# Attention and two MoE stages on one core: the last chunk's down product by seven block products

## The chip, the cores and the metric

One core of a Trainium2 chip runs the whole program. The metric is the device time of an execution in microseconds; the time before is the median of three runs.

## The reference

Clustered attention feeds a gated MoE, and that feeds a second MoE, the stage at hand. It has 1536 tokens of width 512 and four experts with 1024 hidden units:

```python
p = domain_probs / (domain_probs.sum(-1, keepdims=True) + 1e-09)
out = np.zeros((N, D), dtype=np.float32)
for e in range(E):
    h = np.maximum(x @ w1[e], 0.0)
    out += p[:, e:e + 1] * (h @ w2[e])
```

## The kernel before, in words

**Numbers in two parts.** Every float32 operand of a matmul is kept as a high and a low part (names that end in h and l: `hh`, `hl`, `wdh`, `wdl`), and every product is three matmuls: high by high, high by low, low by high. ScalarE writes a high part by a cast (`hi`, L1117), VectorE the low part by a subtraction (`lo`, L1120).

**Chunks.** The second MoE runs over 16 chunks, (2, 0) to (2, 15): four experts with four pieces of 256 hidden units each. A chunk has an *up* product, which makes the 256 hidden rows for all tokens, and a *down* product, which multiplies them by w2 and adds the result to `acc`, the sum of the whole output in SBUF. Tokens stand in three blocks of 512: blocks 0 and 1 (`tb`) hold the output transposed, with four tiles of 128x512 each; the third block holds it by rows, as four *row blocks* of 128 tokens.

**Seven products.** A 2 by 2 product of blocks is made from seven block products in place of eight, with sums of weight blocks (`ws`, made by `block_sums`, L189) and sums of hidden blocks (`ts`, made in `up_seven`, L1142). Up products of (2, 1) to (2, 15) go this way. Down products of (2, 1) to (2, 14) do so in `down_seven` (L1229): each of the seven `product` calls has 2 x 3 matmuls, and between them stand the four `last_block` calls (L1263), one for each row block, with 6 matmuls each. The last chunk, (2, 15), uses `up_seven` without the hidden sums (`blocks` is false) and then the plain `down` (L1395): row blocks first, then the four tiles of block 1, then those of block 0, the last tile in two halves.

**How results reach `acc`.** In `down_seven` a result is taken out of PSUM by VectorE, which adds it to `acc` (`by_v`, L1250), or by ScalarE, which copies it to a tile `ev`, from which a transfer issued by GpSimd adds it to `acc` in memory (`by_a`, L1256; an *accumulating transfer*). The four row blocks go by ScalarE with the token's share as scale, and an accumulating transfer. `ev` tiles come in turn from a pool with two buffers and one with three. In the plain `down` VectorE adds everything, and SP issues a store of each finished tile to `out` (L1428).

**Order.** The schedule is written by hand: each engine runs its instructions in the order in which the code issues them, and each DMA queue belongs to an engine (SP for loads and stores, GpSimd for accumulating transfers). An instruction that waits keeps those behind it on its engine waiting. `step()` calls put side work, the next weights' casts above all, between the products.

Of the kernel before, what the change touches and what calls it, by code (L numbers as in the profile page):

```python
# [39 lines left out]
def tile_cluster_attention_moe(ctx, tc, qk, vt, cent, consts, wm1, wm2, probs, probs_t, out):  # L40
# [12 lines left out]
    wtie = const.tile([128, NCL], BF16, name="wtie")  # L53
    zero1 = const.tile([128, 1], F32, name="zero1")
    cT = const.tile([128, H, 2, NCL], F32R, name="cT")
    identb = const.tile([128, 128], BF16, name="identb")
# [166 lines left out]
    def w_steps(todo):  # L223

        prev = None
        for k, part, o, _ in todo:
# [5 lines left out]
            blocks = k[1] not in (0, E2 * NC2 - 1) if part == "d" else k[1] > 0  # L232
# [53 lines left out]
    def attention():  # L286
        with ExitStack() as ax:
            qkp = ax.enter_context(tc.tile_pool(name="qkp", bufs=2))
            stg = ax.enter_context(tc.tile_pool(name="stg", bufs=1))
            clp = ax.enter_context(tc.tile_pool(name="clp", bufs=1))  # L290
            sm = ax.enter_context(tc.tile_pool(name="sm", bufs=2))
# [537 lines left out]
    def moe():  # L829
# [9 lines left out]
        prs = ap_.tile([128, 128], F32, name="prs")  # L839
# [4 lines left out]
        late = []  # L844
        x3_t = [hp1.tile([128, 2, 768], F32R, name="xt" + x) for x in "hl"]
# [112 lines left out]
        def third_seven(key):  # L958
# [4 lines left out]
            x = tp.tile([128, 512], F32, tag="sg", name="sx", bufs=3)  # L963
            y = ev_.tile([128, 512], F32, tag="ev", name="sy")
# [13 lines left out]
            A.copy(out=y[:, 256:512], in_=gc)  # L978
# [8 lines left out]
            add(y[:, 256:512], ga)  # L987
# [154 lines left out]
        def up_seven(key):  # L1142


            blocks = key[1] < E2 * NC2 - 1
# [18 lines left out]
            parts = [([t[:, i * 256:i * 256 + 256] for t in f1], g) for i, g in ((0, ga), (1, y[:, 256:512]))]  # L1164
# [10 lines left out]
            if not blocks:  # L1175
                hi(h12, u2)
            next(t3)
            if blocks:
                ts[1] = [wp.tile([128, 512], F32R, tag="wb", name="th", bufs=2) for _ in range(2)]
                minus(m1, u2, m1)  # L1180
                hi(ts[1], m1)
# [9 lines left out]
            if blocks:  # L1191
                lo(ts[1], m1)
                minus(u2, m5, u2)
            relu_lo(key, 0, x)
            if blocks:
                minus(x, m5, m1)
            relu_part(*parts[1])
            if blocks:
                hi(ts[3], u2)
                hi(ts[2], x)  # L1200
                lo(ts[2], x)
                lo(h22, m5)
            else:
                lo(h12, u2)
                lo(h22, m5)
# [323 lines left out]
```

## Time and profile before

| | |
|---|---|
| median of three runs | 1027.23 us (1026.77 to 1029.91) |
| the profiled execution | 1029.32 us, span 1027.5 us |
| PE | busy 1015.4 us, 99% of the span |
| VectorE (DVE), ScalarE (ACT), GpSimd (POOL) | 82%, 62%, 34% |
| chain that ended last | PE 77%, DVE 5%, POOL 5%, DMA 4%, ACT 3% |
| granted TensorE clock | 0.998 of full speed over the span |
| stores to `out` by SP | 11 of 256 KB and 2 of 128 KB |
| accumulating transfers of 256 KB by GpSimd | 164, median 4.7 us to landing |

PE's busy share is that of pipelined matmuls: a matmul of 512 columns has a duration of 0.39 us, while the next one starts 0.23 us after it. Times of rows are counted from the span's start. A store or transfer lands when its completion is signalled.

### The profile page before, as it was taken

What the parts mean: (1) busy time and instruction counts of PE and PEld (TensorE: products, weight loads), DVE (VectorE), ACT (ScalarE), POOL (GpSimd) and SP (SyncE); (2) the same over time, 40 slices, a digit from 0 to 9 for tenths busy, and PEclk for the clock granted to TensorE, in tenths of its full rate; (3) what the DMA queues carried; (4) which work ended last, traced back from release to release, by engine and by line L of the source; (5) the groups of instructions that cost most, each with busy time, mean ns of one, the idle gap of its engine ahead of it and who ended that gap; (6) DMA issues with size and microseconds to landing.
All of it is one profiled execution on the core that took longest, in us unless ns stands there. A gap on an engine that the chain in (4) does not pass through costs nothing.

```text
span 1027.5 us, 15450 instructions
## 1 busy us (share of the span) xinstructions
PE 1015.4 (99%) x5273; PEld 832.2 (81%) x5273; DVE 842.5 (82%) x1583; ACT 637.4 (62%) x1273; POOL 350.6 (34%) x404
## 2 busy tenths in 40 slices
PE   8999999999999999999999999999999999999998
PEld 5787777787888888788888888888888888888886
DVE  7888888898588887878787888898888889888876
ACT  6788778887566555645544656565565656556561
POOL 2856786652200102010100144433344443334430
PEclk9999999999999999999999999999999999999999
DMA  8677968831713525253410176655667665665753
GB/s 209 173 168 154 192 155 186 196 86 51 201 57 99 126 82 107 85 136 86 101 42 21 41 144 123 144 105 115 125 139 154 131 124 105 130 126 124 144 103 122
DMA packets 62101, 126.27 MB, mean 123 GB/s; under 512 B 16064, under 2 KB 21504, under 8 KB 62024
## 3 DMA queue, kind: packets, MB, share of 16 engines
q0 software_dynamic: 35632, 62.93, 33.6%
q1 hardware_dynamic: 26104, 62.30, 20.5%
q8 instruction: 41, 0.67, 0.3%
q14 instruction: 36, 0.29, 0.1%
q10 hardware_dynamic: 288, 0.07, 0.0%
HBM read 69.47 MB, written 3.21 MB: 71 GB/s over the span
## 4 chain that ended last, share of the span: by engine, by line
PE 77%; DVE 5%; issue 5%; POOL 5%; DMA 4%; ACT 3%; SPq 0%; POOLq 0%; ACTq 0%; DVEq 0%
PE pa L1005 17%; PE pd L1377 9%; PE pd L1242 9%; PE pb L275 6%; PE pb L1297 5%; PE pt L1005 5%; PE ps L495 4%; PE pb L1005 4%; PE pa L275 3%; PE ps L472 2%; PE ps L473 2%; PE pd L1421 2%; DMA raw<-in_qk 2%; PE pv L525 2%; PE pv L530 2%
## 5 line engine op out<-in xcount | busy, mean ns | idle before, releaser
L1260 POOL DMA_DIRECT2D acc<-ev x84 | 73.8, 1026 | 188.0 <-ACT ev L1259 186.5
L478 DVE CUSTOM_DVE_ANT_0 junk<-ps,zero 128x768 bf16<-128x768 f32 x96 | 91.0, 948 | 14.4 <-PE ps L473 13.8
L489 ACT ACTIVATE P<-ps,nm 128x768 f32<-128x768 f32 x96 | 87.4, 910 | 12.7 <-DVE nm L478 12.5
L1383 POOL DMA_DIRECT2D acc<-ev x24 | 20.8, 867 | 202.3 <-ACT ev L1382 202.0
L495 PE MATMUL ps<-ident,P 128*128 128x128 f32 x576 | 84.5, 274 | 0.9 <-ACT sc L443 0.9
L514 DVE TENSOR_TENSOR lo<-ps,hi 128x384 fp32r<-128x384 f32 x128 | 68.8, 554 | 10.5 <-ACT hi L500 8.2
L495 PEld LDWEIGHTS ps<-ident,P 128*128 128x128 f32 x576 | 66.0, 141 | 10.2 <-ACT hi L500 2.5
L1253 DVE TENSOR_TENSOR acc<-pd,acc 128x512 f32<-128x512 f32 x112 | 71.7, 682 | 0.0
L472 PE MATMUL ps<-t 80*128 80x512 f32 x192 | 70.5, 367 | 1.2 <-ACT P L489 0.4
L500 ACT CAST hi<-ps 128x384 fp32r<-128x384 f32 x128 | 58.0, 482 | 18.8 <-PE ps L495 18.5
L1268 POOL DMA_DIRECT2D acc<-ev x56 | 48.3, 886 | 61.6 <-ACT ev L1267 58.1
L473 PE MATMUL ps<-t 128*128 128x512 f32 x192 | 62.3, 345 | 0.0
L1005 PE MATMUL pa<-xsh,wuh 128*128 128x512 f32 x150 | 60.5, 404 | 0.1
L337 POOL TENSOR_TENSOR t<-raw,t 64x768 fp32r<-64x768 f32 x26 | 47.4, 1824 | 35.6 <-DVE lo L514 19.2
L1005 PE MATMUL pa<-xsl,wuh 128*128 128x512 f32 x150 | 59.1, 394 | 0.0
L1005 PE MATMUL pa<-xsh,wul 128*128 128x512 f32 x150 | 59.0, 393 | 0.0
L1005 PE MATMUL pa<-xh,wuh 128*128 128x512 f32 x150 | 58.7, 392 | 0.0
L1005 PE MATMUL pa<-xh,wul 128*128 128x512 f32 x150 | 58.6, 390 | 0.0
L1005 PE MATMUL pa<-xl,wuh 128*128 128x512 f32 x150 | 58.3, 389 | 0.0
L1377 PE MATMUL pd<-hl,wdh 128*128 128x512 f32 x144 | 56.2, 390 | 0.2 <-DVE hl L1055 0.2
L1377 PE MATMUL pd<-hh,wdh 128*128 128x512 f32 x144 | 56.1, 390 | 0.0
L1377 PE MATMUL pd<-hh,wdl 128*128 128x512 f32 x144 | 56.1, 389 | 0.0
(318 smaller groups left out, 3287.7 us busy)
## 6 DMA issues: line engine op xcount, KB each, us to landing
acc<-ev POOLq DMA_DIRECT2D x164, 256.0 KB, 4.7
wraw<-in_wm SPq DMA_DIRECT2D x68, 512.0 KB, 3.9
t<-in_qk POOLq DMA_DIRECT2D x13, 768.0 KB, 6.8
t<-in_qk POOLq DMA_DIRECT2D x14, 384.0 KB, 7.9
raw<-in_qk SPq DMA_DIRECT2D x26, 192.0 KB, 6.8
x<-x SPq DMA_DIRECT2D x21, 192.0 KB, 4.9
R<-rd SPq DMA_DIRECT2D x16, 192.0 KB, 5.3
out<-acc SPq DMA_DIRECT2D x11, 256.0 KB, 2.0
```

What stands on the lines that cost most here:

```text
L275: T.matmul(out=ps, lhsT=w[:, o:o + 128], rhs=x, start=(k == 0 and m == 0), stop=(k == 3 and m == 2))
L472: T.matmul(out=ps, lhsT=t2[:, 0, qs], rhs=t2[:, 1, ks], start=True, stop=False)
L473: T.matmul(out=ps, lhsT=t1[:, 0, qs], rhs=t1[:, 1, ks], start=False, stop=True)
L478: V.tensor_tensor_reduce(out=junk, in0=S_t[n], in1=zero1.to_broadcast([128, S]), scale=-0.125, scalar=3.0e38, op0=ALU.add, op1=ALU.min, ac ...
L489: A.activation(out=P_t[n], in_=S_t.pop(n), func=ACTF.Exp, scale=0.125, bias=nm_t.pop(n), accum_out=rs_t[p][:, h, c:c + 1])
L495: T.transpose(ps[:, i * 128:(i + 1) * 128], P_t[3 * u + i][:, j * 128:(j + 1) * 128], ident)
L514: V.tensor_tensor(out=lo, in0=ps, in1=hi.bitcast(F32), op=ALU.subtract)
L1005: T.matmul(out=ps, lhsT=w[:, o:o + 128], rhs=r, start=first and i == 0 and m == 0, stop=i == 1 and m == 2, skip_group_check=not first)
L1242: T.matmul(out=ps[s], lhsT=w[i][:, o + s * 128:o + s * 128 + 128], rhs=x[j], start=first and m == 0, stop=m == 2, skip_group_check=not first)
L1253: V.tensor_tensor(out=y, in0=ps, in1=y, op=ALU.add)
L1260: G.dma_start(out=acc1[:, 2 * half + s, tb * 512:(tb + 1) * 512], in_=ev, accum_op=ALU.add)
L1377: T.matmul(out=ps, lhsT=w[:, o:o + 128], rhs=x[:, f, sl], start=(n == 0), stop=(n == len(terms) - 1))
```

## The change

The last chunk goes by seven in its down product too. Its up product makes the hidden sums, its down weights get their sums (`w_steps`), and `down_seven` has rules for this chunk (`last`): a tile that will not be added to again (`done`) is stored by SP as soon as it is finished; `by_a` tiles that are done are added by GpSimd (an add of 128x512 in SBUF) in place of an accumulating transfer; the first two row blocks still go by ScalarE and an accumulating transfer, with a store behind each; the third and fourth are scaled and added by VectorE, the fourth in two halves. The plain `down` keeps only the form for (2, 0). The third block's two sums (`sx`, `sy`) get tiles of their own in place of buffers of the two `ev` pools. `cT`, `identb` and `wtie` move to a pool that lives only during the attention, and `prs` becomes a part of `sy`.

```diff
@@ w_steps
-            blocks = k[1] not in (0, E2 * NC2 - 1) if part == "d" else k[1] > 0
+            blocks = k[1] > 0
@@ moe, third_seven
+        sums3 = hp1.tile([128, 512], F32, name="sx"), hp1.tile([128, 256], F32, name="sy")
+        prs = sums3[1][:, 0:128]
...
-            x = tp.tile([128, 512], F32, tag="sg", name="sx", bufs=3)
-            y = ev_.tile([128, 512], F32, tag="ev", name="sy")
+            x, y = sums3
@@ up_seven: what stood under "if blocks" stands for every chunk
-            if not blocks:
-                hi(h12, u2)
...
-            if not blocks:
-                c21()
-                lo(h21, t21)
@@ down_seven
+            last = key == chunks[-1]
...
+            def send(half, tb, s, done):
+                if last and done:
+                    SY.dma_start(out=out[4 * tb + 2 * half + s], in_=acc1[:, 2 * half + s, tb * 512:(tb + 1) * 512])
+
-            def by_v(half, tb):
+            def by_v(half, tb, done=False):
                 def finish(ps, s):
                     y = acc1[:, 2 * half + s, tb * 512:(tb + 1) * 512]
                     V.tensor_tensor(out=y, in0=ps, in1=y, op=ALU.add)
+                    send(half, tb, s, done)
                 return finish
 
-            def by_a(half, tb):
+            def by_a(half, tb, done=False):
                 def finish(ps, s):
                     ev = ev_tile()
                     A.copy(out=ev, in_=ps)
-                    G.dma_start(out=acc1[:, 2 * half + s, tb * 512:(tb + 1) * 512], in_=ev, accum_op=ALU.add)
+                    y = acc1[:, 2 * half + s, tb * 512:(tb + 1) * 512]
+                    if last and done:
+                        G.tensor_tensor(out=y, in0=ev, in1=y, op=ALU.add)
+                        send(half, tb, s, done)
+                        return
+                    G.dma_start(out=y, in_=ev, accum_op=ALU.add)
                 return finish
 
             def last_block(t):
                 ps = bank("b")
+                if last and t > 1:
+                    for cs in [slice(0, DM)] if t == 2 else [slice(0, 256), slice(256, DM)]:
+                        y = acc1[:, t, 1024 + cs.start:1024 + cs.stop]
+                        ps = bank("b") if cs.start else ps
+                        rows_(ps[:, cs], h, raw, t, cs)
+                        V.scalar_tensor_tensor(out=y, in0=ps[:, cs], scalar=pn[:, t, e:e + 1], in1=y, op0=ALU.mult, op1=ALU.add)
+                        SY.dma_start(out=out[8 + t, :, cs], in_=y)
+                    return
                 rows_(ps, h, raw, t, slice(0, DM))
                 ev = ev_tile()
                 A.activation(out=ev, in_=ps, func=ACTF.Copy, scale=pn[:, t, e:e + 1])
                 G.dma_start(out=acc1[:, t, 1024:1536], in_=ev, accum_op=ALU.add)
+                if last:
+                    SY.dma_start(out=out[8 + t], in_=acc1[:, t, 1024:1536])
...
             last_block(0)
             product(u, sums, 256, ts[2], False, by_v(0, 1))
...
-            product(q, sums, 768, b22, False, by_a(0, 1))
+            product(q, sums, 768, b22, False, by_a(0, 1, True))
             next(rest)
             last_block(1)
-            product(u, sums, 512, ts[3], False, by_a(1, 1))
+            product(u, sums, 512, ts[3], False, by_a(1, 1, True))
             step()
-            product(q, raw, DM, b21, True, by_v(0, 0))
+            product(q, raw, DM, b21, True, by_v(0, 0, True))
             step()
             last_block(2)
-            product(u, raw, DM + 256, ts[4], False, by_v(1, 0))
+            product(u, raw, DM + 256, ts[4], False, by_v(1, 0, True))
             step()
             last_block(3)
```

Two places of the instruction order follow, with what each instruction waits for in brackets. A name that begins with DMASW is the completion of an accumulating transfer, one with DMAHW that of a load or store eight issues earlier, `DVE`, `Pool` and `Activation` are instructions of those engines.

SP's stores at the end of the program, before:

```order
L1428 DMA out<-acc 128x512 [waits DMAHW7_49,DVE_49]
L1428 DMA out<-acc 128x512 [waits DMAHW0_49,DVE_49]
L1428 DMA out<-acc 128x512 [waits DVE_49] x2
L1428 DMA out<-acc 128x512 [waits DMASW3_49,DVE_49]
L1428 DMA out<-acc 128x512 [waits DMASW4_49,DVE_49]
L1428 DMA out<-acc 128x512 [waits DMAHW5_49,DMASW5_49,DVE_49]
L1428 DMA out<-acc 128x512 [waits DMAHW6_49,DMASW6_49,DVE_49]
L1428 DMA out<-acc 128x512 [waits DMAHW7_49,DVE_49]
L1428 DMA out<-acc 128x512 [waits DMAHW0_49,DVE_49]
L1428 DMA out<-acc 128x512 [waits DMAHW1_49,DVE_49]
L1428 DMA out<-acc 128x256 [waits DMAHW2_49,DVE_49]
L1428 DMA out<-acc 128x256 [waits DMAHW3_49,DVE_49]
```

and in the change, where L1278 is the store of row blocks 0 and 1, L1242 that of a tile of blocks 0 and 1, and L1271 that of row blocks 2 and 3:

```order
L1278 DMA out<-acc 128x512 [waits DMAHW7_49,DMASW5_49]
L1242 DMA out<-acc 128x512 [waits DMAHW0_49,DMASW3_49,Pool_49]
L1242 DMA out<-acc 128x512 [waits DMASW4_49,Pool_49]
L1278 DMA out<-acc 128x512 [waits DMASW6_49]
L1242 DMA out<-acc 128x512 [waits Pool_49] x2
L1242 DMA out<-acc 128x512 [waits DMAHW5_49,DVE_49]
L1242 DMA out<-acc 128x512 [waits DMAHW6_49,DVE_49]
L1271 DMA out<-acc 128x512 [waits DMAHW7_49,DVE_49]
L1242 DMA out<-acc 128x512 [waits DMAHW0_49,DVE_49]
L1242 DMA out<-acc 128x512 [waits DMAHW1_49,DVE_49]
L1271 DMA out<-acc 128x256 [waits DMAHW2_49,DMASW2_49,DVE_49]
L1271 DMA out<-acc 128x256 [waits DMAHW3_49,DVE_49]
```

The number of stores is the same. The first waits for an accumulating transfer of the same chunk (DMASW5), two for GpSimd, the fourth for a second accumulating transfer (DMASW6), and nine stand behind that one.

GpSimd's end of the program, before (the last rows are those of chunk (2, 14)):

```order
L1260 DMA acc<-ev 128x512 [waits DMASW5_49,DVE_49,Activation_49]
L1268 DMA acc<-ev 128x512 [waits DMASW6_49,Activation_49]
L1260 DMA acc<-ev 128x512 [waits DMASW7_49,Activation_49]
L1260 DMA acc<-ev 128x512 [waits DMASW0_49,Activation_49]
L1268 DMA acc<-ev 128x512 [waits DMASW1_49,Activation_49]
L1268 DMA acc<-ev 128x512 [waits DMASW2_49,Activation_49]
```

and in the change, where these rows (with L1276 for L1268) are followed by the last chunk's:

```order
L192 TENSOR_TENSOR ws<-wraw 128x256 [waits DMAHW6_49,DVE_49,Pool_49]
L193 TENSOR_TENSOR ws<-ws,wraw 128x256 [waits Pool_49]
L195 TENSOR_TENSOR ws<-wraw 128x256 [waits DVE_49]
L196 TENSOR_TENSOR ws<-wraw,ws 128x256 [waits Pool_49]
L1260 DMA acc<-ev 128x512 [waits DMASW3_49,Activation_49]
L1260 DMA acc<-ev 128x512 [waits DMASW4_49,Activation_49]
L1276 DMA acc<-ev 128x512 [waits DMASW5_49,Activation_49]
L1257 TENSOR_TENSOR acc<-ev,acc 128x512 [waits DVE_49,Activation_49] x2
L1276 DMA acc<-ev 128x512 [waits DMASW6_49,Activation_49]
L1257 TENSOR_TENSOR acc<-ev,acc 128x512 [waits Activation_49] x2
```

GpSimd had nothing to do in the last chunk; now it makes the weight sums, issues four accumulating transfers (L1276 those of row blocks 0 and 1) and makes four adds (L1257), two of them between the two transfers of the row blocks.

## Rows read from the trace of the kernel before

**Rows 1.** The page's first part: busy us, share of the span, instructions.

```profile
PE 1015.4 (99%) x5273; PEld 832.2 (81%) x5273; DVE 842.5 (82%) x1583; ACT 637.4 (62%) x1273; POOL 350.6 (34%) x404
```

**Rows 2.** Chain of waits, in order of time, its end: start us, us, what.

```profile
1007.10 6.02 PE pd L1297 x24
1013.12 10.96 PE pd L1421 x54
...
1024.11 0.42 DVE acc L1426
```

**Rows 3.** Timeline of PE, last chunk: start us, us, instruction, idle before.

```profile
1006.43 0.40 PE L1005 MATMUL pa<-xsh,wul 128*128 128x512 f32 x1
1007.10 0.50 PE L1297 MATMUL pd<-wdh,hh 128*128 128x512 f32 x1 [0.27 <-ACT hh L1129]
...
1023.79 0.28 PE L1421 MATMUL pd<-hh,wdl 128*128 128x256 f32 x1
```

**Rows 4.** Timeline of PE, chunk (2, 14).

```profile
962.07 0.39 PE L1005 MATMUL pa<-xh,wuh 128*128 128x512 f32 x1
...
976.84 0.40 PE L1242 MATMUL pd<-hh,wdh 128*128 128x512 f32 x1
...
989.16 0.50 PE L1242 MATMUL pd<-hh,wdh 128*128 128x512 f32 x1
...
992.03 0.39 PE L1005 MATMUL pa<-xh,wuh 128*128 128x512 f32 x1
```

**Rows 5.** SP's waits from 990 on: us in total, times, longest.

```profile
SPq L1428 <- DVE acc L1416: 42.2, 4, 41.4
SPq L1428 <- DVE acc L1426: 6.8, 8, 0.9
SPq L1523 <- DMA out<-acc: 1.2, 3, 0.5
```

**Rows 6.** L1428's stores: all; landing of the one at 1015.2; of the last.

```profile
L1428 SPq DMA_DIRECT2D out<-acc x13: 332/332/360, 1012.0 to 1024.6; - x13
...
DMA to landing us min/median/max: 2.0/2.0/2.0
...
DMA to landing us min/median/max: 1.7/1.7/1.7
```

**Rows 7.** Timeline of GpSimd (POOL), chunk (2, 14).

```profile
985.15 0.86 POOL L1268 DMA_DIRECT2D acc<-ev  x1 [2.87 <-ACT ev L1267]
986.00 1.77 POOL L1260 DMA_DIRECT2D acc<-ev  x2
988.11 0.86 POOL L1268 DMA_DIRECT2D acc<-ev  x1 [0.34 <-ACT ev L1267]
```

**Rows 8.** GpSimd's adds by line: busy us, mean ns, idle before.

```profile
L194 POOL TENSOR_TENSOR ws<-wraw 128x256 f32<-128x256 f32 x14 | 16.4, 1171 | 78.7 <-DVE wul L259 78.7
...
L589 POOL TENSOR_TENSOR x<-x,x 128x768 f32<-128x768 f32 x7 | 12.7, 1820 | 4.2 <-DMA x<-x 4.2
...
L195 POOL TENSOR_TENSOR ws<-ws,wraw 128x256 f32<-128x256 f32 x14 | 10.7, 764 | 1.1
```

**Rows 9.** Timeline of ScalarE (ACT), chunk (2, 14).

```profile
985.12 1.07 ACT L1259 COPY ev<-pd 128x512 f32<-128x512 f32 x2
...
988.52 1.07 ACT L1259 COPY ev<-pd 128x512 f32<-128x512 f32 x2 [0.70 <-DMA acc<-ev]
```

**Rows 10.** L1268's accumulating transfers: landing of the one at 985.1; at 988.1.

```profile
DMA to landing us min/median/max: 3.3/3.3/3.3
...
DMA to landing us min/median/max: 4.6/4.6/4.6
```

**Rows 11.** Stretches: busy us of each engine, PE clock, DMA share, GB/s.

```profile
1013.50:1014.50 1.00, 1.00 (x6) 0.84 (x5) 0.43 (x1) 0.00 (x0) 0.00 (x0) 1.00 1.05 408
1014.50:1015.50 1.00, 1.00 (x6) 0.81 (x6) 0.69 (x1) 0.00 (x0) 0.00 (x0) 1.00 0.99 381
```

**Rows 12.** Timeline of VectorE (DVE), chunk (2, 14).

```profile
987.30 0.69 DVE L1120 TENSOR_TENSOR hl<-t,hh 128x512 fp32r<-128x512 f32 x1
```

More of the change, by code (lines that the diff above doesn't have):

```diff
@@ L977, in third_seven @@
             A.copy(out=x[:, 0:256], in_=ga)
-            A.copy(out=y[:, 256:512], in_=gc)
+            A.copy(out=y, in_=gc)
             yield x, y, ga
@@ L986, in third_seven @@
             prod(key, ga, S_(3), t_(3), False)
-            add(y[:, 256:512], ga)
+            add(y, ga)
             yield
@@ L1163, in up_seven @@
             f1 = h_blk(key, 1, 2)
[L1164 removed]
+            parts = [([t[:, i * 256:i * 256 + 256] for t in f1], g) for i, g in ((0, ga), (1, y))]
             prod(key, pa, S_(2), T_(2), False)
@@ L1174, in up_seven @@
             relu_p(key, u2, u2, 1)
-            if not blocks:
-                hi(h12, u2)
             next(t3)
[L1178 to L1181, printed above, removed]
+            ts[1] = [wp.tile([128, 512], F32R, tag="wb", name="th", bufs=2) for _ in range(2)]
+            minus(m1, u2, m1)
+            hi(ts[1], m1)
             prod(key, pa, S_(3), T_(3), False)
@@ L1274, in down_seven @@
             h_t.pop(key)
-            if (key[1] + 1) % NC2 == 0:
+            if (key[1] + 1) % NC2 == 0 and not last:
                 share_load(e + 1)
@@ L1399, in down @@
             e = key[1] // NC2
-            first = key[1] == 0
-            cuts = [(tb, t, slice(0, 512)) for tb in ((1, 0, 2) if first else (2, 1, 0)) for t in range(4)]
-            if not first:
-                cuts[-1:] = [(*cuts[-1][:2], slice(i * 256, (i + 1) * 256)) for i in range(2)]
-            for tb, t, cs in cuts:
-                if first:
-                    ensure((2, "x1" if tb < 2 else "x2"))
-                ps = down_banks[0].tile([128, 512], F32, tag="d", name="pd")[:, cs]
-                sl = slice(tb * 512 + cs.start, tb * 512 + cs.stop)
-                y = acc1[:, t, sl]
-                if tb == 2:
-                    rows_(ps, h, w, t, cs)
-                    pe = pn[:, t, e:e + 1]
-                    if first:
-                        A.activation(out=y, in_=ps, func=ACTF.Copy, scale=pe)
-                    else:
-                        V.scalar_tensor_tensor(out=y, in0=ps, scalar=pe, in1=y, op0=ALU.mult, op1=ALU.add)
-                else:
-                    for f in range(FC):
-                        for m, (i, j) in enumerate(((0, 0), (0, 1), (1, 0))):
-                            o = f * DM + t * 128
-                            T.matmul(out=ps, lhsT=w[i][:, o:o + 128], rhs=h[j][:, f, sl], start=(f == 0 and m == 0),
-                                     stop=(f == FC - 1 and m == 2))
-                    if first:
-                        A.copy(out=y, in_=ps)
-                    else:
-                        V.tensor_tensor(out=y, in0=ps, in1=y, op=ALU.add)
-                if not first:
-                    SY.dma_start(out=out[4 * tb + t, :, cs], in_=y)
-                step()
@@ new lines, in down @@
+            for tb in (1, 0, 2):
+                ensure((2, "x1" if tb < 2 else "x2"))
+                for t in range(4):
+                    ps = down_banks[0].tile([128, 512], F32, tag="d", name="pd")
+                    sl = slice(tb * 512, (tb + 1) * 512)
+                    y = acc1[:, t, sl]
+                    if tb == 2:
+                        rows_(ps, h, w, t, slice(0, DM))
+                        A.activation(out=y, in_=ps, func=ACTF.Copy, scale=pn[:, t, e:e + 1])
+                    else:
+                        for f in range(FC):
+                            for m, (i, j) in enumerate(((0, 0), (0, 1), (1, 0))):
+                                o = f * DM + t * 128
+                                T.matmul(out=ps, lhsT=w[i][:, o:o + 128], rhs=h[j][:, f, sl], start=(f == 0 and m == 0),
+                                         stop=(f == FC - 1 and m == 2))
+                        A.copy(out=y, in_=ps)
+                    step()
@@ L1473, in moe @@
                     down(k)
-                elif i + 1 < len(chunks):
+                else:
                     down_seven(k, *up_seven(k))
-                else:
-                    up_seven(k)
-                    down(k)
     with tc.manual_schedule():
```

31 lines of the change are left out of this document (12 added, 19 removed).

## The prediction

> **What bounds the kernel now.** The page's first part shows TensorE (PE) busy for 99% of the span [rows 1]; a change is worth something only if it shortens PE's own row of matmuls or what follows the last of them. The chain of waits says the same of the end: it ends with 24 and 54 matmuls of the last chunk's down product and one VectorE add [rows 2]. The PE timeline dates it: the up product's last matmul is issued at 1006.43 and would be followed 0.23 us later, at 1006.66, but the down product, which waits for a ScalarE relu, starts at 1007.10, 0.44 us late, and its last 256-column matmul starts at 1023.79 [rows 3]. Call 1006.66 the *start of the down*; the span ends 20.84 us after it. What the changed chunk will look like stands in the chunk before it, (2, 14), which goes by seven already: its down starts at 976.84 without a pause, is held up a little at 989.16 (a matmul of 0.50 us where 0.39 is usual), and is followed at 992.03: 15.19 us for 66 matmuls of 512 columns [rows 4]. A time of chunk (2, 14) plus 29.82 us (1006.66 less 976.84) is the same place in the last chunk.
>
> The end of the span is not PE's alone. SP issues 13 stores, in order; in the kernel before each waits for VectorE's adds [rows 5]. They start at 1012.0 and keep up with the engines, so just the last one stands behind the last matmul. A 256 KB store lands 2.0 us after its issue, a 128 KB one 1.7 us [rows 6]. The last one, issued at 1024.6, has landed at 1026.3, 1.2 us ahead of the end of the span.
>
> **The change part by part.** The profiled execution has a span of 1027.5 us and took 1029.32 us; the median of the three runs is 1027.23, 2.1 us less. I work out the difference within the span and add it to the median.
>
> *PE.* The last down has 72 matmuls of 512 columns (two rows of 256 count as one); seven products and four row blocks make 42 + 24 = 66. Taking chunk (2, 14) as the model, the late start goes too. The last 12 matmuls have 256 columns, and the last of them starts about 0.12 us before the end of those 15.19 us, at 1006.66 + 15.07 = 1021.73 instead of 1023.79: **2.06 us earlier**. The two weight sums, their ScalarE casts and VectorE lows, and GpSimd's four adds for them come back in the last up. Chunk (2, 14) carries the same, with the next chunk's weights besides: its up took 14.77 us (962.07 to 976.84) against 14.63 in the last chunk (992.03 to 1006.66), so at most 0.14 us. The pool shift and the own tiles of the third block's sums remove waits that were over long before, and none of them ended a wait of PE; I put them at nothing. What covers the sums is PE's own work, behind which ScalarE and VectorE write them in each up; with that cover gone, PE would be held up as at 989.16, by about 0.1 us in each of 15 chunks, 1.5 us.
>
> *GpSimd.* In chunk (2, 14) GpSimd issues the accumulating transfer of the first row block at 985.15, two more at 986.00, and that of the second row block at 988.11 [rows 7]. In the changed last chunk the two in the middle become adds of 128x512, and GpSimd works in order: the second row block's transfer now stands behind two whole adds. No such add is in the trace. The nearest rows are 1.82 us for 128x768 and 0.76 to 1.17 us for 128x256 [rows 8]; 512 columns lie halfway between, at 1.3 us, which I take; the bounds are 1.2 (two thirds of 1.82) and 1.8 (as dear as 768 columns). The inputs are there in time: the ScalarE copies of chunk (2, 14) start at 985.12 [rows 9]. So the adds run from 986.0 to 988.6, and the second row block's transfer is issued at 988.6, that is at **1018.4** in the last chunk. It lands 3.3 us later when alone, 4.6 us when others are moving [rows 10]; here three stores of 256 KB move at the same time, and I take 4.0: **1022.4** (1021.7 to 1023.0).
>
> *SP.* This is where I expect the time to go. SP's row now begins with the store of the first row block, which must wait for that block's accumulating transfer (985.15 + 29.82 + 3.3 = 1018.3) instead of going at 1012. After two stores that wait for GpSimd comes the store of the second row block, which waits for the transfer that lands at 1022.4. Behind it, in order, stand nine stores: four tiles of the second and first blocks, the third row block, two tiles of the last product and two halves of the fourth row block. Nearly all of these are ready before 1022.5. Ten stores are then issued in a bunch, at 0.33 us each [rows 6], and hold 8 x 256 KB + 2 x 128 KB = 2.36 MB. The busiest stretches of the end moved 408 and 381 GB/s at a full DMA share [rows 11]; at 395 the bunch takes 6.0 us, plus 1.34 us that a store needs beside its bytes (2.0 less 0.66). The last lands at 1022.4 + 1.3 + 6.0 = 1029.7, and with the 1.2 us at the end the span is **1030.9**, 3.4 us longer. PE's 2.06 us are covered by this and gain nothing.
>
> [...]
>
> *ScalarE.* Its last two copies move banks that the last product accumulates into. In chunk (2, 14) the copy at 988.52 waited 0.70 us for a transfer to free its buffer [rows 9]; in the change that buffer is freed by the second GpSimd add, at about 988.6. That is 0.1 us on PE, hidden like PE's gain.
>
> **Forecast:** 1027.23 + 3.4 = **1030.6 us**, slower by 0.33%. Bounds of this case: with 3.3 for the landing (0.7 less) and the rate that the two landings imply, 128 KB in 0.3 us or 437 GB/s (0.6 less), and 1.2 for each add (0.2 less), +1.9 us; with 1.8 for each add (1.0 more) and 4.6 for the landing (0.6 more), +5.0 us. So 1029.1 to 1032.2.
>
> **The rivals.**
>
> *The stores are not held up: not slower.* If the store of the second row block doesn't keep those behind it waiting (its transfer lands early, or later stores pass it), only PE counts: the last matmul starts 2.06 us earlier, less 0.1 for the copy, and the same tail follows. That gives 1027.23 - 1.95 = 1025.3 us. The point from which it decides: the bunch ends as early as the old stores did if the transfer lands by 1022.4 - 3.4 = 1019.0, only 0.6 us after its issue as worked out here. For it: SP before never waited for a landing, so no row shows a store held up by one. Against: stores before waited for VectorE one after the other [rows 5], and the shortest landing of this transfer is 3.3 us [rows 10].
>
> *The GpSimd adds are much dearer.* On GpSimd one and the same kind of 128x256 add takes 0.76 or 1.17 us, 1.53 times as much, by its place [rows 8]. At 1.3 x 1.53 = 2.0 us each the second row block's transfer is issued 1.4 us later, and with the 4.6 us landing (0.6) the end is at +5.4: 1032.6 us. The trace does not say what makes the dear ones dear. [...]
>
> *The change doesn't do what it says:* the weight sums arrive late for the second product, PE pauses, and the saving of six matmuls is gone. Chunk (2, 14) does the same work with more beside it and starts its down without a pause [rows 4]; and if it pauses by up to 2 us, the bunch of stores hides that. So this has no price of its own.
>
> **How the numbers follow.** About 0.3%, 3.1 us, is what a measurement of this kernel can tell from no change. The forecast's case has a chance of 0.74, the rival without held-up stores 0.14, the dear adds 0.12. The forecast's case lies from +1.9 to +5.0 with its middle at 3.4, so some 0.44 of its 0.74 is slower by over 3.1 and 0.30 is within. Slower is 0.44 + 0.12 = 0.56. The first rival lies at -1.95, within the bound, but for 0.04 that the scatter of three runs (1026.77 to 1029.91) could carry past it: faster 0.04, same 0.40. Both sides of zero hold much of the chance, so the range reaches from the first rival, 1025.0, to just above the dear adds, 1033.0; the likeliest case's own range is 1029.1 to 1032.2.
>
> **What would show it.** Right, if after the change SP issues a store at about 1018, then stands until about 1022, and then issues ten within 4 us; if the DMA share is full from there to about 1029; if PE's last matmul starts near 1021.8, and the span ends over 6 us behind it; if the GpSimd adds take about 1.3 us. Wrong, if SP's row shows no wait of more than 2 us for an accumulating transfer, or if the last store is issued less than 1 us behind the last VectorE operation. If the adds take 2 us, the second rival holds.

## The result, and the profile after

In five runs each, beside one another on one chip, the change takes 1034.76 us (median, 1033.27 to 1036.56) and the kernel before 1027.52: a ratio of 1.0070, 95% interval 1.0058 to 1.0082. The forecast was 1030.6 us, with a range from 1025.0 to 1033.0. The direction is right; the forecast rise of 3.4 us is about half of the measured 7.2. The profiled execution took 1036.56 us, with a span of 1034.4.

The page's first part, for [rows 1]:

```profile
PE 1013.1 (98%) x5267; PEld 831.1 (80%) x5267; DVE 846.9 (82%) x1590; ACT 643.9 (62%) x1286; POOL 362.7 (35%) x416
```

PE issues six matmuls fewer and is busy for 2.3 us less, yet the span is 6.9 us longer. The timeline of PE in the last chunk, for [rows 3], shows that the saving was there and was partly lost:

```profile
1008.22 0.39 PE L1007 MATMUL pa<-xsh,wul 128*128 128x512 f32 x1
1008.46 0.39 PE L1232 MATMUL pd<-hh,wdh 128*128 128x512 f32 x1
...
1022.30 0.50 PE L1232 MATMUL pd<-hh,wdh 128*128 128x512 f32 x1 [1.42 <-ACT ev L1254]
...
1025.11 0.28 PE L1307 MATMUL pb<-wdh,hl 128*128 128x256 f32 x1
```

The start of the down is 1008.45 here (1008.22 + 0.23), and no pause precedes it. The last matmul starts 16.66 us later, where the prediction had 15.07. Before the last product PE stands for 1.42 us, waiting for a bank that ScalarE copies out. To see why ScalarE is late, read VectorE, GpSimd and ScalarE of the same stretch together. VectorE's timeline:

```profile
1016.13 0.68 DVE L1122 TENSOR_TENSOR hl<-t,hh 128x512 fp32r<-128x512 f32 x1
1016.85 3.68 DVE L1128 TENSOR_TENSOR t<-t,sx 128x512 f32<-128x512 f32 x1
1021.21 0.69 DVE L1122 TENSOR_TENSOR hl<-t,hh 128x512 fp32r<-128x512 f32 x1 [0.69 <-ACT hh L1119]
...
1023.68 1.27 DVE L1247 TENSOR_TENSOR acc<-pd,acc 128x512 f32<-128x512 f32 x2
```

GpSimd's timeline, for [rows 7]:

```profile
1016.56 0.86 POOL L1276 DMA_DIRECT2D acc<-ev  x1 [2.54 <-ACT ev L1275]
1017.12 2.85 POOL L1257 TENSOR_TENSOR acc<-ev,acc 128x512 f32<-128x512 f32 x2
1022.37 0.87 POOL L1276 DMA_DIRECT2D acc<-ev  x1 [2.40 <-ACT ev L1254]
1022.97 2.82 POOL L1257 TENSOR_TENSOR acc<-ev,acc 128x512 f32<-128x512 f32 x2
```

ScalarE's timeline, for [rows 9]:

```profile
1020.56 0.62 ACT L1119 CAST hh<-t 128x512 fp32r<-128x512 f32 x1 [3.34 <-DVE t L1128]
1021.09 0.68 ACT L1275 ACTIVATE ev<-pb,pn 128x512 f32<-128x512 f32 x1
1021.67 1.06 ACT L1254 COPY ev<-pd 128x512 f32<-128x512 f32 x2
```

VectorE's subtraction `t<-t,sx`, whose two operands both lie in SBUF, takes 3.68 us while GpSimd's first two adds run; an instruction of the same shape beside no add takes 0.68 (1016.13). In e1_pad and e4_store_order, which leave the adds there, it takes 3.67 and 3.68. ScalarE's cast of that `t` waits for it (idle for 3.34 us), behind the cast in ScalarE's row stands the activation of the second row block, and behind that the copies that PE waits for. So the second row block's accumulating transfer is issued at 1022.37, 13.9 us after the start of the down instead of the 11.7 of the prediction (1018.4 less 1006.66), although the adds had ended at about 1020.0.

From there SP's row goes as forecast. Its timeline, for [rows 6]:

```profile
1019.85 0.34 SPq L1278 DMA_DIRECT2D out<-acc  x1
1020.29 0.87 SPq L1242 DMA_DIRECT2D out<-acc  x2
1025.66 0.33 SPq L1278 DMA_DIRECT2D out<-acc  x1
1026.05 2.01 SPq L1242 DMA_DIRECT2D out<-acc  x4
1028.15 0.60 SPq L1271 DMA_DIRECT2D out<-acc  x1
1028.84 1.28 SPq L1242 DMA_DIRECT2D out<-acc  x2
1030.22 1.27 SPq L1271 DMA_DIRECT2D out<-acc  x2
```

SP's waits from 990 on, for [rows 5], now name the transfer, and no longer VectorE:

```profile
SPq L1278 <- DMA acc<-ev: 52.2, 2, 47.7
```

Of the 52.2 us, 47.7 are the wait for the first row block; the other 4.5 are the stand before 1025.66, the moment at which the second row block's transfer has landed (1022.37 + 3.3). The ten stores then issue in a bunch. Stretches of that time, for [rows 11] (us, busy us of PE, PEld, DVE, ACT, POOL, PE's granted clock, DMA share, GB/s):

```profile
1024.00:1026.00 2.00, 1.39 (x12) 1.18 (x10) 1.83 (x4) 0.00 (x0) 1.79 (x2) 1.00 0.64 109
...
1028.00:1030.00 2.00, 0.00 (x0) 0.00 (x0) 0.00 (x0) 0.00 (x0) 0.00 (x0) 0.96 1.03 382
1030.00:1032.00 2.00, 0.00 (x0) 0.00 (x0) 0.00 (x0) 0.00 (x0) 0.00 (x0) 0.50 1.02 381
```

The DMA share is full from 1028 to 1032, at 382 and 381 GB/s, long after the last engine has stopped. PE's granted clock is 1.00 from 1006 to 1026, as long as PE works, so the clock is no part of it. The span ends 25.95 us after the start of the down, where it was 20.84.

That explains 5.1 us of 6.9. The span can be cut into three stretches: up to the first matmul of the first MoE's down ("attention"), from there to the start of the last down ("middle"), and the tail behind it. The table has them in us, from one profiled execution each, for the twelve further kernels too; the next section says what each of those is.

| kernel | attention | middle | tail |
|---|---|---|---|
| before | 289.1 | 717.6 | 20.84 |
| the change | 291.4 | 717.0 | 25.95 |
| e1_pad, e11_pad_again | 287.9, 287.8 | 717.0, 717.3 | 25.62, 25.6 |
| e6_again, e12_change_again | 292.9, 289.4 | 716.7, 716.5 | 25.92, 26.01 |
| e2_moves_only | 289.7 | 716.7 | 20.78 |
| e10_moves_pad | 287.4 | 716.3 | 20.69 |
| e5_before_shift | 291.3 | 718.0 | 20.87 |
| e3_vector_adds | 287.4 | 717.1 | 24.07 |
| e4_store_order | 290.1 | 716.1 | 24.32 |
| e7_adds_behind | 292.3 | 716.1 | 24.22 |
| e8_best | 288.2 | 716.8 | 20.83 |
| e9_rows_first | 288.8 | 716.3 | 23.26 |

In the change the attention is 2.4 us longer, the middle 0.6 shorter. The attention of single profiled executions scatters by as much as 3.5 us (the change itself: 291.4, 292.9, 289.4), so there the medians below decide; its tail repeats within 0.1 us.

Two theories followed. **Hold-up and queue:** the tail's 5.1 us are the bunch of stores and VectorE's subtraction, held up by GpSimd's adds. **Placement:** moving `cT` (1024 bytes a partition), `identb` (256) and `wtie` (32) out of the constants, 1312 bytes = 5 x 256 + 32, sets the tiles behind them that transfers read and write 32 bytes below a multiple of 256 bytes (below, such kernels are called shifted), and the attention's transfers become slower. The rivals were that GpSimd's adds are dear by themselves, that the own tiles cost the time, and that the attention only scatters.

### The profile page after: what moved, and what is told of

The parts are those of the page before. It is cut to its first block, busy times and chain, and to the rows that moved or that the text cites. A ratio compares the mean times of both kernels' runs of the same rounds, so it can differ in the third digit from the quotient of the medians.

```text
span 1034.4 us, 15456 instructions
## 1 busy us (share of the span) xinstructions
PE 1013.1 (98%) x5267; PEld 831.1 (80%) x5267; DVE 846.9 (82%) x1590; ACT 643.9 (62%) x1286; POOL 362.7 (35%) x416
## 3 DMA queue, kind: packets, MB, share of 16 engines
q0 software_dynamic: 36208, 63.98, 34.9%
## 4 chain that ended last, share of the span: by engine, by line
PE 77%; DMA 7%; POOL 4%; issue 4%; DVE 4%; ACT 2%; SPq 0%; ACTq 0%; POOLq 0%; DVEq 0%
PE pa L1007 18%; PE pd L1232 11%; PE pd L1387 9%; PE pb L1307 6%; PE pt L1007 6%; PE pb L273 6%; PE pb L1007 4%; PE ps L497 3%; PE pa L273 3%; DMA raw<-in_qk 2%; DMA x<-x 2%; PE ps L474 2%; PE ps L475 2%; PE pv L532 1%; PE pv L527 1%
## 5 line engine op out<-in xcount | busy, mean ns | idle before, releaser
L1260 POOL DMA_DIRECT2D acc<-ev x86 | 75.6, 1026 | 198.7 <-ACT ev L1254 197.2
L1393 POOL DMA_DIRECT2D acc<-ev x24 | 20.6, 858 | 202.2 <-ACT ev L1392 202.1
L1247 DVE TENSOR_TENSOR acc<-pd,acc 128x512 f32<-128x512 f32 x120 | 76.7, 679 | 0.0
L1276 POOL DMA_DIRECT2D acc<-ev x58 | 50.1, 908 | 68.1 <-ACT ev L1275 62.2
L339 POOL TENSOR_TENSOR t<-raw,t 64x768 fp32r<-64x768 f32 x26 | 47.4, 1824 | 37.7 <-DMA raw<-in_qk 34.4
```

The costliest lines, as they stand in the source:

```text
L1260: G.dma_start(out=y, in_=ev, accum_op=ALU.add)
```

## The experiments

Every ratio is to the kernel before on the same chip; e1 to e4, e5 to e8 and e9 to e12 each share one chip.

**e1_pad and e11_pad_again.** The change, with an unused constant of 32 bytes that puts the tiles back on multiples of 256; the second time beside the change itself.

```diff
     cT = identb = wtie = None
+    const.tile([128, 8], F32, name="pad")
```

> The change, plus an unused tile of 32 bytes per partition behind the constants, so that the tiles that transfers read and write (x, the loads' t, raw and vs, acc, wraw) stand on multiples of 256 bytes again, as before; in the change they stand 32 bytes below one. Theory A (moving cT, identb and wtie out of the constants costs, by where the tiles then stand): the down product of the first MoE starts at 289, not 291.4 us, the accumulating transfers' share of the DMA engines goes back from 34.9% to about 33.6%, and the median falls by about 2 us, to 1032.5. Rival (the 2.4 us of the attention are the scatter of single runs): the median stays at 1034.8 within 0.6. The end is unchanged under both: about 26 us from the start of the last down to the end of the span.

> e1_pad once more, on the chip of the change beside it. Theory A: 1.5 to 3 us under e12_change_again, with an end only 0.3 us shorter. Rival (chips and scatter): within 0.8 us of it.

Measured: 1031.94 us, 1.0033 [1.0021, 1.0044], and 1032.78 us, 1.0040 [1.0027, 1.0054].

**e6_again and e12_change_again.** The change without an edit, as the partner of e7 and e8 and of e11.

> The change once more, unedited, on the same chip as the kernels beside it, to stand against e1_pad and e3_vector_adds. Theory A: about 1034.3, 2 us above e1_pad's 1031.9 where its end is only 0.3 us longer. Rival: 1032.3 within 0.6, e1_pad's time plus the 0.3 us; then the change's first time held 2 us of scatter. The end is 25.6 to 26.0 us behind the start of the last down under both, with the subtraction at 3.7 us.

> The change unedited, on the chip of e11_pad_again. Theory A: 1.5 to 3 us above e11_pad_again, and 5.5 to 7 above the kernel before. Rival: within 0.8 us of e11_pad_again.

Measured: 1034.89 us, 1.0058 [1.0044, 1.0072], and 1034.33 us, 1.0055 [1.0038, 1.0072]. On one chip the 32 unused bytes are worth 1.55 us (1034.33 less 1032.78). The two intervals overlap, so this pair alone doesn't settle it. PE's waits in the attention, e12 first and then e11 (us in total, times, longest):

```profile
PE ps L474 <- DMA t<-mk: 2.6, 3, 1.6
```

```profile
PE ps L475 <- DMA t<-mk: 0.5, 1, 0.5
```

It is the transfers of `t` out of `mk` that PE waits for more often. Before: 0.4 us, once. These waits scatter too (1.1 us in the shifted e5, 1.0 in the padded e10). Steadier is the time that the transfers themselves take. The queue of those that GpSimd issues, over the whole span, e12 first and then e11 (packets, MB, share of the 16 engines' time):

```profile
q0 software_dynamic: 36208, 63.98, 34.8%
```

```profile
q0 software_dynamic: 36208, 63.98, 34.0%
```

For the same bytes the shifted change, e6 and e12 have 34.9, 34.8 and 34.8%, the padded e1 and e11 34.1 and 34.0; with the 62.93 MB of before it is 34.1 (e5) and 34.4 (e2) against 33.6 (before) and 33.7 (e10). So the transfers do take more time where the tiles are shifted.

**e5_before_shift.** The kernel before, with 224 unused bytes among its constants, the same remainder as in the change (32 below a multiple of 256), and nothing else of it.

```diff
     pn = const.tile([128, NL, E2], F32, name="pn")
+    const.tile([128, 56], F32, name="pad")
```

> The kernel before with an unused tile of 224 bytes per partition behind the constants, so that x, the loads' tiles, acc and wraw stand 32 bytes below a multiple of 256, as in the change; nothing else differs. Theory A (where the tiles stand costs): 1 to 2.5 us slower than before, all of it in the attention (the first MoE's down product starts 1 to 2.5 us later on the mean; a single profile scatters by 2 us), and the transfers' share of the DMA engines is higher by 0.5 to 1 point. Rival (no such cost): the same as before within 0.6 us.

Measured: 1030.69 us, 1.0017 [1.0006, 1.0029], 1.7 us slower than before with not one instruction changed; the attention is 2.2 us longer, the middle (718.0) and the tail (20.87) are nearly as before. PE's waits for `t<-mk` are 1.1 us.

**e2_moves_only and e10_moves_pad.** The kernel before with the moved constants and the third block's own tiles, last chunk untouched; e10 adds e1's 32 bytes.

```diff
-    wtie = const.tile([128, NCL], BF16, name="wtie")
...
+    cT = identb = wtie = None
...
+            wtie = clp.tile([128, NCL], BF16, name="wtie")
...
+        sums3 = hp1.tile([128, 512], F32, name="sx"), hp1.tile([128, 256], F32, name="sy")
...
-            y = ev_.tile([128, 512], F32, tag="ev", name="sy")
+            x, y = sums3
```

> The kernel before with only the moved constants and the own tiles of the third block's sums; its last chunk goes by the plain down product. Theory A: about 2 us slower than before, 1029.5, all of it ahead of the first MoE's down product. Rival (scatter): 1027.5, the same as before. A third reading, that the own tiles cost something in each chunk of the second MoE, would show as a longer stretch from the first MoE's down product (289.1 before) to the start of the last down (1006.7 before): over 717.6 us.

> e2_moves_only plus 32 bytes of padding: moved constants and own tiles, with the tiles on multiples of 256 bytes again and the plain last down. Theory A with a gain of the own tiles (the stretch from the first MoE's down product to the last down was 716.1 to 717.1 us in all kernels with own tiles, 717.6 and 717.9 without): 0.5 to 1.5 us under the kernel before. Rival (own tiles gain nothing, where the tiles stand costs nothing): the same as before within 0.5 us, and the stretch is 717.5 or more.

Measured: 1028.95 us, 1.0005 [0.9997, 1.0014], and 1027.64 us, 0.9990 [0.9979, 1.0001]. e2 missed its 2 us: its interval holds 1. Between the two kernels, on different chips, lie 1.3 us, which fits the cost of the placement, and the rest of this part seems to give something back: the middle is 0.9 and 1.3 us under before's 717.6, and it is shorter than before's in all kernels with the own tiles (716.1 to 717.3), while e5 without them has 718.0. In the attention the five padded kernels lie at 287.4 to 288.8 and seven of the eight shifted ones at 289.4 or more; e3, shifted too, has 287.4 and before, on multiples of 256, 289.1, so single profiles only lean one way, and the verdict rests on the medians and on the transfers' share above.

**e3_vector_adds.** The four tiles that GpSimd finishes go to VectorE instead, straight from PSUM; ScalarE's copies of them go too.

```diff
-                    ev = ev_tile()
-                    A.copy(out=ev, in_=ps)
                     y = acc1[:, 2 * half + s, tb * 512:(tb + 1) * 512]
                     if last and done:
-                        G.tensor_tensor(out=y, in0=ev, in1=y, op=ALU.add)
+                        V.tensor_tensor(out=y, in0=ps, in1=y, op=ALU.add)
                         send(half, tb, s, done)
                         return
+                    ev = ev_tile()
+                    A.copy(out=ev, in_=ps)
```

> The change with the four adds of finished tiles made by VectorE straight from PSUM, none by GpSimd. Theory B (the GpSimd adds hold up VectorE's subtraction t<-t,sx, which took 3.68 us beside them and 0.69 us in the chunk before; ScalarE and the second row block's transfer stand behind it): the subtraction takes 0.69 us again, that transfer is issued 3 to 4 us earlier, at 11 us behind the start of the down and not at 13.9, PE's pause of 1.4 us ahead of the last product goes, and the median falls by 2.5 to 3.5 us, to about 1031.8. Rival C (VectorE's subtraction waits for something else, a transfer or PSUM): it stays above 3 us, and with four more adds on VectorE the end is no earlier than the change's, 1034.8 or more. The bunch of stores behind the second row block's stays under both: ten stores within 4 to 6 us, the DMA share full for 6 us.

Measured: 1032.20 us, 1.0039 [1.0025, 1.0053]; tail 24.07. The same subtraction in VectorE's timeline, and the second row block's transfer in GpSimd's:

```profile
1012.93 0.69 DVE L1128 TENSOR_TENSOR t<-t,sx 128x512 f32<-128x512 f32 x1
```

```profile
1015.46 0.86 POOL L1276 DMA_DIRECT2D acc<-ev  x1 [1.96 <-ACT ev L1275]
```

Without adds on GpSimd the subtraction takes 0.69 us, the transfer goes 10.9 us after the start of the down instead of 13.9, and the tail is 1.9 us shorter. What is left is 3.2 us over before, and SP's row shows the queue in it: e3's SP still stands until that transfer lands and then issues ten stores,

```profile
1016.36 1.29 SPq L1242 DMA_DIRECT2D out<-acc  x2
1019.87 0.33 SPq L1278 DMA_DIRECT2D out<-acc  x1
...
1024.43 1.28 SPq L1271 DMA_DIRECT2D out<-acc  x2
```

**e7_adds_behind.** The same adds on GpSimd, but the first two are issued behind the second row block's transfer.

```diff
                     if last and done:
-                        G.tensor_tensor(out=y, in0=ev, in1=y, op=ALU.add)
-                        send(half, tb, s, done)
+                        def add():
+                            G.tensor_tensor(out=y, in0=ev, in1=y, op=ALU.add)
+                            send(half, tb, s, done)
+                        behind.append(add) if half == 0 else add()
                         return
...
                 if last:
+                    for fn in behind:
+                        fn()
```

> The change with its first two GpSimd adds put behind the second row block's accumulating transfer on GpSimd's queue; the same adds, the same stores in the same order. Theory B (a GpSimd add holds up a VectorE operation that reads two operands from SBUF, and nothing that reads one from PSUM): the subtraction takes 0.69 us, the second row block's transfer is issued at about 11 us behind the start of the down (13.9 in the change, 10.9 with VectorE's adds), and VectorE's adds from PSUM stay at 0.68 us beside the GpSimd adds. The four adds, 1.4 us each, then end at about 17.5, and seven stores stand behind the last of them: the end is at about 24 us, 1.5 to 2 less than the change's 25.9. Rival C: the subtraction stays at 3.7 us and the end at 25.9.

Measured: 1033.96 us, 1.0045 [1.0033, 1.0057]; tail 24.22. VectorE's timeline, then GpSimd's:

```profile
1016.77 0.69 DVE L1128 TENSOR_TENSOR t<-t,sx 128x512 f32<-128x512 f32 x1
...
1021.73 1.39 DVE L1247 TENSOR_TENSOR acc<-pd,acc 128x512 f32<-128x512 f32 x2
```

```profile
1019.30 0.86 POOL L1280 DMA_DIRECT2D acc<-ev  x1 [1.96 <-ACT ev L1279]
1019.87 5.30 POOL L1260 TENSOR_TENSOR acc<-ev,acc 128x512 f32<-128x512 f32 x4
```

All four adds are still there and hardly cheaper (5.30 us, 1.33 each), and yet the subtraction takes 0.69 us and PE has no pause. So it is neither the adds' own length nor their number; what differs is what VectorE had beside them. In the change that was a subtraction with two SBUF operands (3.68 us); here it is adds with one operand in PSUM, 0.7 us each, which are hardly held up (1.39 us for two, 1.28 for two beside no add at 1012.47).

**e4_store_order.** The change, with the stores of the second row block and of the two tiles of `by_a(1, 1)` put behind those of the last product.

```diff
-                if last and done:
+                if last and done and (half, tb) == (1, 1):
+                    held.append(...)
+                elif last and done:
...
-                if last:
+                if last and t:
+                    held.append(...)
+                elif last:
...
             product(u, raw, DM + 256, ts[4], False, by_v(1, 0, True))
             step()
+            for fn in held[1:] + held[:1]:
+                fn()
             last_block(3)
```

> The change with three stores, those of the second row block and of the two tiles of by_a(1, 1), put on SP's queue behind the last product's, ahead of the fourth row block's halves. Theory D (the store of the second row block keeps nine finished ones waiting on SP's in-order queue): stores begin to leave at about 1022.5 on the scale of the change's trace and not at 1025.7, the transfers have a head start of 2 to 3 us, and the median falls by 1.5 to 2.5 us, to about 1032.8. Rival (the stores are bound by what VectorE and GpSimd finish, and the queue's order costs nothing): 1034.8 within 0.6.

Measured: 1032.90 us, 1.0044 [1.0029, 1.0060]; tail 24.32, 1.6 us shorter than the change. VectorE's subtraction is held up as before (3.68 us), so PE's pause stays:

```profile
1014.68 3.68 DVE L1128 TENSOR_TENSOR t<-t,sx 128x512 f32<-128x512 f32 x1
```

Each of the two cures takes 1.6 to 1.9 us off the tail, and neither alone brings it back.

**e8_best.** Both cures and the 32 bytes: `by_a(0, 1)` is added by VectorE out of PSUM, the second row block and `by_a(1, 1)` by GpSimd adds (no accumulating transfer stands in front of a store), and the stores are issued in the order in which their tiles are ready.

```diff
+                    if last and done and half == 0:
+                        V.tensor_tensor(out=y, in0=ps, in1=y, op=ALU.add)
+                        send(half, tb, s, done)
+                        return
...
+                if last and t:
+                    G.tensor_tensor(out=y, in0=ev, in1=y, op=ALU.add)
+                    held.append(...)
+                    return
...
+            release(1)
             last_block(2)
+            release(1)
             product(u, raw, DM + 256, ts[4], False, by_v(1, 0, True))
             step()
+            release(1)
```

> The change with 32 bytes of padding; the tiles of by_a(0, 1) added by VectorE from PSUM; those of by_a(1, 1) and the second row block added by GpSimd, when no VectorE operation with two SBUF operands is left; SP's stores in the order in which their tiles are ready. All theories together: no operation is held up, PE's last matmul starts 15.1 to 15.4 us behind the start of the down, stores leave from 9.8 us on, and the end is bound by the 3.15 MB of stores, 8 us at 390 GB/s: 19.7 to 21 us against 20.84 before, 25.9 in the change. Median 1027.0 to 1028.5 where the kernel before has 1028.3. Rival (the queue's order and the hold-up are not the cause): an end above 23 us.

Measured: 1028.34 us, 0.9991 [0.9980, 1.0002], 6.5 us under the change on the same chip, and not to be told from the kernel before. Its tail is 20.83, although its last matmul starts 15.38 us after the start of the down, 1.75 earlier than before's 17.13. Stretches of its end:

```profile
1016.00:1018.00 2.00, 2.00 (x10) 1.65 (x9) 1.33 (x4) 0.43 (x1) 2.00 (x2) 1.00 0.94 360
1018.00:1020.00 2.00, 2.00 (x14) 1.80 (x13) 2.00 (x3) 0.00 (x0) 1.72 (x2) 1.00 1.06 409
1020.00:1022.00 2.00, 0.73 (x7) 0.52 (x5) 0.99 (x3) 0.00 (x0) 0.00 (x0) 1.00 1.05 404
1022.00:1024.00 2.00, 0.00 (x0) 0.00 (x0) 0.00 (x0) 0.00 (x0) 0.00 (x0) 1.00 1.05 391
```

Now the transfers end the kernel: a full share at about 400 GB/s from 1018 to 1024. Before, VectorE's adds finished tiles from 1012 on, and the stores filled the share only for single us [rows 11]; over 2 us it was 0.76 at most. That the seven products finish their tiles too late for the stores is the reading of this; e9 was to test it.

The split of the tail's 5.1 us depends on what is cured first: without the hold-up the queue costs 3.2 us (e3), with the queue in order the hold-up still costs some 3.5 (e4's 24.32 against e8's 20.83, which also takes one accumulating transfer out).

In e8 a VectorE subtraction with two SBUF operands meets one of GpSimd's adds after all:

```profile
1015.34 0.68 DVE L1123 TENSOR_TENSOR hl<-t,hh 128x512 fp32r<-128x512 f32 x1
```

```profile
1015.55 1.64 POOL L1287 TENSOR_TENSOR acc<-ev,acc 128x512 f32<-128x512 f32 x1 [1.45 <-ACT ev L1284]
```

Here the subtraction keeps its 0.68 us and the add is the longer one: 1.64 us, where the two adds behind it take 1.28 each.

**e9_rows_first.** To finish tiles earlier, with e1's 32 bytes: all four row blocks directly behind the first two products, through ScalarE and accumulating transfers; every tile of the later products is added by VectorE.

```diff
+            if last:
+                product(u, raw, 0, b11, True, by_a(0, 0))
+                product(q, sums, 0, ts[1], True, by_v(1, 1))
+                next(rest)
+                last_block(0)
+                last_block(1)
...
+                last_block(2)
+                next(rest)
+                last_block(3)
...
+                product(u, raw, DM + 256, ts[4], False, by_v(1, 0, True))
+                return
```

> The change with 32 bytes of padding and another order in the last down: after the first two products all four row blocks, by ScalarE and accumulating transfers, then the other five products, whose finished tiles are all added by VectorE from PSUM; no GpSimd add; stores in the order of readiness. If the end is bound by how late the seven products finish their tiles (the stores of e8_best filled the transfers from 1016 to 1024), four of the twelve tiles are now ready by about 12.5 us behind the start of the down and not the last ones: PE's last matmul starts at 15.1, the last store lands at about 18, the end is at 18.8 to 20.2 us against 20.84 before and 20.83 in e8_best, and the median is 1 to 3 us under that of the kernel before. Rival (the accumulating transfers of the row blocks hold the stores back as the second one did): 21 us or more.

Measured: 1030.04 us, 1.0015 [1.0003, 1.0028], tail 23.26: a miss. Its stretches:

```profile
1010.00:1012.00 2.00, 2.00 (x11) 1.65 (x10) 1.67 (x3) 1.10 (x3) 1.55 (x2) 1.00 0.89 154
1012.00:1014.00 2.00, 2.00 (x11) 1.65 (x10) 1.39 (x2) 1.52 (x3) 1.59 (x2) 1.00 1.12 198
...
1022.00:1024.00 2.00, 0.00 (x0) 0.00 (x0) 0.00 (x0) 0.00 (x0) 0.00 (x0) 1.00 1.06 410
```

Until the first store is issued at 1015.08, accumulating transfers alone take a DMA share of 0.89 and 1.12 at 154 and 198 GB/s, where stores move 410 at 1.06, and from 1012 to 1026 the share stays full (1.04 to 1.12). That they delayed the stores by more than the earlier order gained fits these rows; no run of its own shows it. A version that clearly beats the kernel before was not found.

## Why the prediction was right and wrong

**The store queue: right.** The order of events was as forecast: a store at the first row block's landing, a stand until the second one's, ten stores in a bunch, a full share, the end 1.1 us behind the last landing (1030.9 + 2.4 = 1033.3). With the hold-up taken out (e3), the tail is 24.07 us; the prediction had 1030.9 less 1006.66, or 24.24. Two small misses of opposite sign are in that match: e3's transfer goes at 10.9 instead of 11.7, and its store follows 4.4 us later (1019.87 less 1015.46) instead of 4.0. The first is partly luck: e3 has no adds on GpSimd at all, and without the two adds the prediction's own rows would have put the transfer at 11.3 (988.11 + 29.82 less 1006.66).

**PE: right, but for a pause.** Without a pause the last matmul starts 15.15 us (e7) or 15.38 (e8) after the start of the down, forecast 15.07. e8 also shows that the saving was hidden by the stores, as the prediction said, and that it stays hidden when the queue is in order.

**The step "GpSimd" was wrong.** It priced the adds at 1.3 us (measured 1.42) and looked at what stands behind them on GpSimd's own row alone. What else runs beside them was left out: VectorE's subtraction, 0.69 us, became 3.68, and through ScalarE it delayed the transfer and PE. In the sum's own terms: the transfer 2.2 us later (13.9 against 11.7), its landing 0.7 shorter (3.3 against 4.0), the bunch with its last landing 0.3 longer (1033.3 less 1025.7 = 7.6, against 7.3): 1.8 us, and the tail is 25.95 against 24.24. e3 and e7 show that the overlap is the cause.

The trace of the kernel before had it already. Its L1114 multiplies two tiles in SBUF (`snap`, `pe`); beside GpSimd's weight sums of chunk (2, 14) it reads, VectorE first and then GpSimd:

```profile
965.79 1.20 DVE L1114 SCALAR_TENSOR_TENSOR snap<-snap,pe 128x512 f32<-128x512 f32 x1
```

```profile
965.71 0.74 POOL L197 TENSOR_TENSOR ws<-wraw 128x256 f32<-128x256 f32 x1
966.40 1.19 POOL L198 TENSOR_TENSOR ws<-wraw,ws 128x256 f32<-128x256 f32 x1
```

L1114 takes 0.69 us in the median; it takes 0.90 to 1.28 beside these sums in 10 of the 14 chunks, and in each of the 14 one of GpSimd's sums beside it takes 1.1 to 1.2 us instead of 0.74. The prediction's [rows 8] have these sums as means by line, without what VectorE runs beside them; in the trace both engines are slowed there, VectorE included.

Which of the two is held up differs. In the change it was VectorE: its subtraction ended at 1020.53, 0.56 us behind both adds (1017.12 + 2.85 = 1019.97). In e8 it was GpSimd, with an add of 1.64 us; beside L1114 it was both, 1.20 us and 1.19. The order of the starts doesn't tell the two apart: the subtraction starts 0.21 us ahead of the add in e8 and keeps its time, and 0.27 us ahead of the first add in the change and is held up. GpSimd's records overlap by 0.3 us there (1016.56 + 0.86 = 1017.42), so a lead of that size is not a sure order. What decides it, no run shows.

**The sentence that put the pool shift and the own tiles "at nothing" was wrong twice.** The shift costs 1.3 to 1.7 us in the pairs e2/e10, e11/e12 and before/e5, and more, about 2.5 to 3, if e1 and e6, from different chips, are compared; the own tiles give back about 1 us in the middle. That the shift costs is shown best by e5 (its interval leaves 1 out) and by the transfers' share of the engines' time; that the own tiles gain was read from the middles alone and has no run of its own.

**Sum.** Bunch 3.2, hold-up 1.9, shift about 1.7, own tiles about -1: 5.8 us; the change was 7.2, 5.9 and 6.0 us over the kernel before in the three comparisons. What the first has more, no run explains; its five runs of the kernel before have a lower median (1027.52) than the 23 to 27 runs on the other chips (1028.29 to 1028.99). **The rivals:** stores not held up fell. "GpSimd adds much dearer" came nearest in its time (1032.6), for a wrong reason, as an add took 1.42 us and not 2.0. That the change doesn't do what it says fell too.

**What stays open:** why 32 bytes slow the transfers was not traced below their share of the engines' time and the waits for `t<-mk`. The runs have the tiles on multiples of 256 bytes and 32 below one; what other places cost, and by which mechanism, none shows. Nor is it shown where on PE the own tiles gain.

## What to carry to other kernels

When work is given to GpSimd, list VectorE's instructions with two SBUF operands that run beside it (here one took 3.68 us in place of 0.69), and who waits behind them; to put the adds elsewhere (e7) or to let VectorE make them straight from PSUM (e3) was a cure here: 0.69 us in both. When stores are issued in order on one queue, put them in the order in which their tiles get ready, and keep a tile that waits for an accumulating transfer out of the front (e4: a tail 1.6 us shorter). When a tile leaves a pool, look where the others come to lie, and try the change with the old remainder to 256 bytes restored before its schedule is blamed (here 32 unused bytes were worth 1.55 us, e12 against e11).

## What the runs showed of the hardware that was not expected

- GpSimd's two adds of 128x512 held one VectorE subtraction up from 0.69 to 3.68 us, in the change and in e4; VectorE's adds with one operand in PSUM went on at about 0.7 us beside such adds (e7: 1.39 us for two). In e8 it was the add that took longer, 1.64 us instead of 1.28.
- 224 unused bytes a partition made the kernel before 1.7 us slower (1.0017, interval 1.0006 to 1.0029); the transfers that GpSimd issues took 34.1% of the engines' time instead of 33.6 for the same bytes.
- Accumulating transfers held a full DMA share at 176 GB/s (1.03, the change from 1014 to 1016) and 198 (1.12, e9 from 1012 to 1014); stores moved 382 (1.03, the change from 1028 to 1030) to 410 (1.06, e9 from 1022 to 1024) at such a share.
- In a bunch, a store's issue on SP lengthened from 0.33 us to 0.50 and then about 0.6 (the change: 2.01 us for four, then 0.60, 1.28 and 1.27 for two each).
